# A backward pass with a long convolution and two dense layers: the opening put in one written order on all engines, with three spectrum blocks turned by DMA

## The chip, the cores and the metric

The kernel runs on one core of a Trainium2 chip. The time is device time in microseconds for one execution of the whole program; the median of several runs is given. A profile is one execution taken by the hardware profiler. PE is TensorE's matmul, PEld its weight load, DVE is VectorE, ACT is ScalarE, POOL is GpSimd, SP is SyncE, which here only issues DMAs.

## The reference

Two layer pairs are applied to x = A_q (1 x 2048 x 448, bf16): a gated long convolution A and a dense layer B with SiLU, A and B again; the outputs are the result and the gradients for all weights and inputs.

```python
def _A_ref(q, k, v, shift_k, ssm_k, ssm_D):
    ...
    for t in range(ks):
        k_shift = k_shift + k_pad[:, t:t + S, :] * shift_k[:, ks - 1 - t][None, None, :]
    kv = k_shift * v
    L = 2 * S
    ...
    y_f = kv_f * kf_f[None, :, :, :]
    y = (lambda x, s, axes=(-2,-1): jnp.fft.irfft2(x, s=s, axes=axes).astype(jnp.bfloat16))(y_f, (1, L), axes=(1, 2))[:, 0, :S, :]
    y = y + kv * ssm_D[None, None, :]
    return q * y
...
    x = x + _A_ref(_layernorm(x, axis=-1), A_k, A_v, A_shift_k, A_ssm_k, A_ssm_D)
    x = x + _B_ref(_layernorm(x, axis=-1), B_w1, B_w2)
    x = x + _A_ref(_layernorm(x, axis=-1), A_k, A_v, A_shift_k, A_ssm_k, A_ssm_D)
    x = x + _B_ref(_layernorm(x, axis=-1), B_w1, B_w2)
```

The convolution's result y depends on k, v and the filters alone, so it is computed once, ahead of the layers, by a Fourier transform of length 4096 written as matmuls (2048 = 128 x 16, in two stages).

## The kernel before

`_ssm_prefix` computes y; this text calls the part from the turn of k on (line 426 and after) the opening. `Main` then runs the layers forward and backward in four chunks of 512 rows, and `_ssm_suffix` with `Jobs` the convolution's gradients and the weight gradients.

The prefix begins by loading the filter, the constant matrices M1sb and Gsb, k, v and the first chunk of x (x0c0), all on SP's DMA queue (lines 371 to 380), and transforms the filter by its first stage into KAB's first half (`k_turn`, `k_stage1`). Then comes the opening. Its kinds of work, with the lines of before:

- k is transposed by TensorE into kT (line 432), half of each copy on ACT and half on DVE (434). `conv` (449) applies the four-tap shift as matmuls against diagonal matrices `diag` on half the channels (h) and four of the 16 row groups (jq); ACT copies the result to ks_kv (452), POOL stores it to DRAM (KS_d, 454), DVE multiplies it with v (455).
- `stage1_kv` is the first transform stage of that product (465), written to A1kv; once all jq of one half are in, A1kv is turned in 7 blocks of 16 squares of 128x128 (514) into Zkv (two tiles, ZkvA and ZkvB), where the second stage follows (`_fft_stage2_full`, 244) on 14 pieces of 1024.
- The filter's first stage is likewise turned in 7 blocks: two by DMA (426), five by TensorE in halves of 64 rows (`turn`, 225). `spec_k` (469) runs its second stage, stores the spectrum to DRAM and writes, with four DMAs from SBUF to SBUF (`_swap_halves_dma`, 282), a copy with real and imaginary parts exchanged into KAB's first half.
- `cons_prod` (519) copies a piece of the KV spectrum, stores it (540), has DVE multiply it with both forms of the filter's (pab, 542), and the inverse second stage (253, 254) goes from pab to PSUM and back to A1kv, whose storage is B1.
- In between, the first layer norm of x0c0 runs in eight steps (`_ln_steps`: four of statistics, POOL's power for rstd, four of scaling), and the weights w2T (by a transposing DMA), w1sb and w2sb are loaded.

After it `ys` (563) does the inverse first stage from B1 and ACT copies y to Ysb (564), which takes the buffer of ZkvA; X takes that of ZkvB. All PSUM tiles of the opening rotate through one tag, A, with four buffers. The order of each engine's instructions here is the scheduler's, from program order and priorities; which of ACT and DVE makes a copy is chosen by a running balance (`bal.pick`). From `Main` on, PE's order is that of the program (`manual_schedule`).

Of the kernel before, what the change touches and what calls it, by code (L numbers as in the profile page):

```python
# [17 lines left out]
P = 128  # L18
# [101 lines left out]
KPARTS = [(0, 128), (128, 256), (256, 384), (384, 448)]  # L120

# [126 lines left out]
def _fft_inv_stage2_full(k, pa, pb, B1, ci, psum):  # L248
# [6 lines left out]
    _copy(nc, k.bal.pick(1024), B1[:, 8 * ci:8 * ci + 8, :].rearrange("p a b -> p (a b)"), pv[:].rearrange("p a b -> p (a b)"))  # L255
# [56 lines left out]
def _ln_steps(k, pool, c, src, si, n_g):  # L312
# [4 lines left out]
    for tl in range(4):  # L317
        k.tc.keep_in_program_order(nc.vector.bn_stats(out=st[:, tl, :], in_=src(tl)))
# [15 lines left out]
def _ssm_prefix(k):  # L334
# [4 lines left out]
    with ExitStack() as es:  # L339
# [6 lines left out]
        k.M1sb = k.wk.tile([P, 16, 2, P], BF16, name="M1sb", tag="WX")  # L346
# [71 lines left out]
        def turn(src, dst, g):  # L418
            pt = psum.tile([P, 2, 16, 64], BF16, name="ps_tr", **a_)
            for i in range(16):  # L420
                _turn64(k, pt, i, src[:, 16 * g + i, :])
            for lo, hi, o in dst(g):
                _copy(nc, bal.pick((hi - lo) * P, dve_ns=0.53), o.rearrange("p i (r x) -> p r i x", r=2), pt[:, :, lo:hi, :])

        for g in range(5, 7):
            nc.sync.dma_start_transpose(out=Z[:, 16 * g:16 * g + 16, :], in_=A1Kf[:, 16 * g:16 * g + 16, :].rearrange("p a b -> p (a b)"))
        for jq in range(4):
            pt = psum.tile([DC, ND, 4, P], BF16, name="ps_kT", **a_)
            for u in range(4):
                j = 4 * jq + u  # L430
                for dc in range(ND):
                    nc.tensor.transpose(pt[:, dc, u, :], kn[:, j, dc * DC:(dc + 1) * DC], k.ident[:])
            for e, lo, hi in ((nc.scalar, 0, 2), (nc.vector, 2, 4)):
                _copy(nc, e, kT[:, jq, lo:hi, :, 1:129], pt[:, lo:hi])
        k.w2T = k.wk.tile([P, ND, F], BF16, name="w2T", tag="WY")
        nc.sync.dma_start_transpose(out=k.w2T[:, 0:3, :], in_=k.B_w2[:, 0:384])
        nc.sync.dma_start_transpose(out=k.w2T[:, 3:4, :], in_=k.B_w2[:, 320:448])
        DH = D // 2

        def conv(h, jq):  # L440
            ds = slice(h * DH, (h + 1) * DH)
            pc = psum.tile([P, 4, 256], FP32, name="ps_cv", tag="A", bufs=4)
            for u in range(4):
                j = 4 * jq + u
                for e in range(2):
                    for t in range(4):
                        js = (j - t) % J
                        src = kT[:, js // 4, 2 * h + e, js % 4, 1:129] if j >= t else kT[:, js // 4, 2 * h + e, js % 4, 0:128]
                        nc.tensor.matmul(pc[:, u, e * DC:(e + 1) * DC], lhsT=src, rhs=diag[:, 2 * h + e, t, :], start=(t == 0), stop=(t == 3))  # L449
            kk = work.tile([P, 2, 4, DH], BF16, name="ks_kv", tag="pab", bufs=4)  # L450
            ks, kvt = kk[:, 0], kk[:, 1]
# [41 lines left out]
        for p in prev:  # L493
            stage1_kv(*p)
# [880 lines left out]
```

## Time and profile before

| | us |
|---|---|
| median of 3 runs | 702.56 (701.79 to 702.73) |
| the profiled execution | 701.8 |
| its span | 700.0 |
| the opening in it | 18.9 to 90.6 |
| PE, DVE, ACT, POOL busy over the span | 666.0, 484.1, 432.9, 101.3 |

The span is counted from the execution's first record; times such as "at 41 us" are from there. Busy time is that of the engine's instructions, without waits; a group's row gives the line, engine, operation, output and inputs, shapes, count, then busy us and mean ns of one, then idle time just before and what ended it. A wait's row reads: engine and tile that waited, what it waited for, us in total, times, longest. A DMA's row gives where to and from, the issuing queue, count, KB each, and the median us from issue to landing.

### The profile page before, as it was taken

The page shows a single profiled execution, that of the slowest core. Times are in us where ns is not written, and L with a number is a line of the kernel's source. Part 1 is how long each engine was busy: PE and PEld are TensorE (multiplying, and loading weights), DVE is VectorE, ACT ScalarE, POOL GpSimd, SP SyncE. Part 2 cuts the span into 40 slices and gives each one's busy share as a digit, 9 for nine tenths or more (in the row PEclk, how much of TensorE's full clock was granted, in tenths as well). Part 3 has the DMA queues.
Part 4 walks back from the last instruction along what each step waited for, and adds up shares of the span by engine and source line. Part 5 has one row for each costly group of instructions (what it writes and reads, how often), then busy time and mean ns, then how long its engine had stood idle before and what let it go on. Part 6 is the DMA issues. An engine that isn't in the chain of part 4 may idle for free.

```text
span 700.0 us, 14553 instructions
## 1 busy us (share of the span) xinstructions
PE 666.0 (95%) x5897; PEld 358.8 (51%) x5933; DVE 484.1 (69%) x1131; ACT 432.9 (62%) x522; POOL 101.3 (14%) x173
## 2 busy tenths in 40 slices
PE   6898789999999999999999999999999999999996
PEld 5876545454444444434444444544554555555664
DVE  6688862676889948899578874853946545538991
ACT  5888766968856857769577585223554553554431
POOL 1057110110011100111000100010111211102311
PEclk9999999999999999999999999999999999999999
DMA  8999938459899976698677799959557888966981
GB/s 321 270 298 306 376 84 210 118 107 243 219 231 249 246 200 166 146 240 221 185 165 194 194 242 329 262 172 229 177 208 280 307 279 307 352 188 215 331 293 42
DMA packets 199798, 161.03 MB, mean 230 GB/s; under 512 B 147698, under 2 KB 180213, under 8 KB 198963
## 3 DMA queue, kind: packets, MB, share of 16 engines
q1 hardware_dynamic: 184550, 111.78, 58.8%
q0 software_dynamic: 10368, 36.29, 15.3%
q10 hardware_dynamic: 4812, 12.04, 5.0%
q8 instruction: 46, 0.75, 0.4%
q14 instruction: 22, 0.17, 0.1%
HBM read 66.05 MB, written 54.60 MB: 172 GB/s over the span
## 4 chain that ended last, share of the span: by engine, by line
PE 57%; DVE 22%; issue 10%; ACT 5%; POOL 3%; DMA 2%; POOLq 0%; DVEq 0%; ACTq 0%
PE ps_d L1046 19%; PE ps_n L836 8%; PE ps_h L638 6%; PE ps_g L638 6%; PE ps_o L798 5%; DVE ln_st L301 2%; DVE lb_v L994 2%; PE ps_v L265 2%; PE ps_cv L449 2%; POOL rstd L306 2%; DVE n L309 1%; DVE lb_v L997 1%; DVE lb_v L998 1%; DVE X L802 1%; PE ps_h L642 1%
## 5 line engine op out<-in xcount | busy, mean ns | idle before, releaser
L1046 PEld LDWEIGHTS <-dstat 128*128 128x128 bf16 x896 | 84.0, 98 | 77.8 <-issue 4.0
L836 PE MATMUL ps_n<-w1T,ghT 128*128 128x448 bf16 x448 | 96.6, 353 | 2.0 <-DVE ghT L821 1.7
L798 PE MATMUL ps_o<-w2sb,aT 128*128 128x448 bf16 x448 | 89.2, 353 | 0.7 <-DVE X L802 0.7
L638 PE MATMUL ps_h<-nT,w1sb 128*128 128x512 bf16 (+1 forms) x410 | 83.5, 336 | 2.2 <-ACT Dall L116 1.0
L116 ACT CAST ghT<-ps_g 128x1024 bf16<-128x1024 f32 (+1 forms) x54 | 48.4, 899 | 58.4 <-PE ps_g L642 47.7
L638 PE MATMUL ps_g<-nT,w2T 128*128 128x512 bf16 x317 | 77.9, 379 | 2.2 <-DVE Dall L117 0.5
L836 PEld LDWEIGHTS <-ghT 128*128 128x128 bf16 x448 | 41.4, 98 | 50.7 <-DVE ghT L821 6.7
L798 PEld LDWEIGHTS <-aT 128*128 128x128 bf16 x448 | 43.2, 98 | 41.1 <-issue 2.8
L638 PEld LDWEIGHTS <-w1sb 128*128 128x128 bf16 x420 | 39.2, 98 | 36.7 <-issue 7.2
L781 ACT ACTIVATE aT<-ps_h 128x1024 bf16<-128x1024 f32 (+1 forms) x48 | 44.2, 921 | 19.4 <-PE ps_h L638 10.5
L116 ACT CAST Dall<-ps_h 128x1024 bf16<-128x1024 f32 (+2 forms) x60 | 54.3, 904 | 0.0
L994 DVE SCALAR_TENSOR_TENSOR lb_v<-lb_u,n 128x448 bf16<-128x448 bf16 x60 | 37.2, 620 | 24.6 <-ACT lb_u L840 24.1
L791 ACT ACTIVATE Dall<-Dall 128x1024 bf16<-128x1024 bf16 (+1 forms) x48 | 53.2, 1186 | 0.1
L638 PEld LDWEIGHTS <-w2T 128*128 128x128 bf16 x336 | 31.3, 98 | 42.1 <-issue 7.2
L306 POOL TENSOR_TENSOR rstd<-ln_ve,mhalf 128x2 f32<-128x2 f32 (+1 forms) x24 | 19.9, 831 | 221.1 <-DVE ln_ve L305 221.1
L1046 PE MATMUL ps_d<-X,dstat 128*128 128x448 bf16 x224 | 47.9, 353 | 0.0
L1046 PE MATMUL ps_d<-go,dstat 128*128 128x448 bf16 x224 | 47.2, 353 | 0.0
L1046 PE MATMUL ps_d<-n3m,dstat 128*128 128x448 bf16 x224 | 46.4, 353 | 0.0
L1046 PE MATMUL ps_d<-n1m,dstat 128*128 128x448 bf16 x224 | 46.3, 353 | 0.0
L840 ACT ACTIVATE lb_u<-ps_n,rstd 128x448 bf16<-128x448 f32 x32 | 20.5, 640 | 28.7 <-PE ps_n L836 24.3
L116 ACT CAST A1g<-ps_v 128x1024 bf16<-128x1024 f32 x14 | 14.9, 1066 | 36.5 <-PE ps_v L265 36.5
L802 DVE TENSOR_TENSOR X<-X,ps_o 128x448 bf16<-128x448 bf16 x32 | 19.5, 610 | 21.3 <-PE ps_o L798 21.1
(206 smaller groups left out, 1111.6 us busy)
## 6 DMA issues: line engine op xcount, KB each, us to landing
dstat<-a_d SPq DMA_DIRECT2D x28, 512.0 KB, 5.0
dstat<-g_d SPq DMA_DIRECT2D x28, 512.0 KB, 5.2
a_d<-turned SPq DMA_DIRECT2D x16, 512.0 KB, 3.0
g_d<-turned SPq DMA_DIRECT2D x16, 512.0 KB, 3.2
a_d<-turned SPq DMA_DIRECT2D x16, 384.0 KB, 2.7
g_d<-turned SPq DMA_DIRECT2D x16, 384.0 KB, 3.0
spec_K<-KAB POOLq DMA_DIRECT2D x7, 512.0 KB, 5.4
KAB<-KAB POOLq DMA_DIRECT2D x28, 128.0 KB, 4.6
```

Source lines behind the costliest of these rows:

```text
L116: return nc.scalar.copy(out, in_)
L265: nc.tensor.matmul(pv[:, r ^ (ci & 1), i, :], lhsT=src[ri, i * P:(i + 1) * P], rhs=k.Gsb[ri, g, ri], start=first, stop=not first)
L306: nc.gpsimd.tensor_tensor(out=r[:, lo:hi], in0=ve[:, lo:hi], in1=k.mhalf[:, lo:hi], op=ALU.pow)
L638: self.nc.tensor.matmul(ps, lhsT=w[:, b, ft * P:(ft + 1) * P], rhs=x[:, b], start=(start and b == 0), stop=(stop and b == bs[2]))
L781: self.last_silu = nc.scalar.activation(aT[hh][:, o:o + hi - lo, :], ps(lo, hi), ACT.Silu)
L791: self.nc.scalar.activation(dT[hh][:, o:o + n, :], dT[hh][:, o:o + n, :], ACT.Derivative_silu)
L798: nc.tensor.matmul(po[:, :D], lhsT=aT[ft // 7][:, ft % 7, tl * P:(tl + 1) * P], rhs=self.w2sb[:, ft, :], start=(ft == 0), stop=(ft == NF - 1))
L802: self.last_o = nc.vector.tensor_tensor(out=X[:, t, :], in0=X[:, t, :], in1=po[:, :D], op=ALU.add)
L836: nc.tensor.matmul(pn[:, :D], lhsT=gh[ft // 7][:, ft % 7, tl * P:(tl + 1) * P], rhs=self.w1T[:, ft, :], start=(ft == 0), stop=(ft == NF - 1))
L840: nc.scalar.activation(u0[:], pn[:, :D], ACT.Identity, scale=k.rstd[2 * L + 1][:, t:t + 1], accum_out=cp[:, tl, 0:1])
L994: nc.vector.scalar_tensor_tensor(out=v[:], in0=u0, scalar=-1.0 / D, in1=n_t, op0=ALU.mult, op1=ALU.mult, accum_out=cp[:, 1:2])
L1046: self.nc.tensor.matmul(ps[:, :D], lhsT=st[:, t, :], rhs=mov[:, t, :], start=(first and t == 0), stop=(last and t == NT - 1))
```

## The change

The opening is written as a list of 207 pieces. A token's first letter says the kind, digits which one; a small letter is a copy or ACT's or DVE's step, with a (ACT) or d (DVE) at its end, and x or y ahead of it for the first or second half of a split copy. T turn of k, t its copy; K turn of a filter block, k its copy; C convolution, c its copy and store, m the product with v; S first stage, s its copy; P second stage of the filter, p its copy, Q store and swap; Z turn of a KV block by TensorE, z its copy, D the same by DMA; F second stage of KV, f its copy and store; M product of spectra, V inverse, v its copy; N a step of the layer norm; W0 grad_out's chunk, W1 w2T, W2 w1sb, W3 w2sb.

Within it all engines, SP's and POOL's queues too, keep the list's order. KV blocks 0, 1 and 2 (D0 to D2), which need only the first half of the channels, are turned by DMA on SP's queue, and their F, M and V stand among the convolutions of the second half. The five filter blocks are turned in whole squares. w1sb and w2sb are loaded by SP instead of ACT, w2T behind D2 instead of ahead of the first store. `diag` moves from the filter's tile to that of M1sb; pab has three buffers of its own and ks_kv two, where both shared four. The steps of the layer norm are no longer pinned one by one.

```diff
+OPENING = """
+W0 T0 N0 T1 t0xa t0yd T3 N1 t1xa T2 t1yd t3xa t3yd C01 t2xa t2yd N2 C02 c01 N3 m01 K1 c02 N4 S011 k1a m02 S010 s011d
+S021 N5 s010a P3 s021d P2 p3a S020 p2d P10 s020a P11 N6 C03 Q1 p10a p11d N7 C00 c03 Q5 m03 P12 c00 S030 p12d P13 s030a
+S031 m00 K4 p13a s031d S001 Q6 S000 s001a k4d K0 s000a P8 k0d P9 p8a D0 K2 p9d P1 P0 p1a k2d Q4 C11 D1 p0a C13 c11 Q0
+m11 D2 P4 c13 P5 p4d S111 p5a S110 m13 K3 s110a s111d Q2 S131 s131a k3d S130 F0 s130a f0d P7 P6 p7a F3 p6d F2 f3a F1 M0
+C10 Q3 f2a M3 f1a C12 c10 M1 V0 m10 c12 V1 M2 v0a S101 v1a m12 V3 s101d S120 v3a V2 s120d S100 v2a S121 W1 W2 W3 s100d
+F4 s121a F5 f4d f5a Z5 M4 Z6 z5a Z4 M5 Z3 z4a z6d V4 z3xd V5 v4a z3yd F12 v5a F7 f12d F11 f7a F13 f11d F10 f13a F9 M7 F8
+f9a F6 M13 f10a f8a M11 V7 f6a V13 M10 V11 v7a M6 V10 v13a M12 V6 v10a M9 V12 v11a M8 v12a V9 v6a v9d V8 v8a
+"""
...
-    _copy(nc, k.bal.pick(1024), B1[:, 8 * ci:8 * ci + 8, :].rearrange("p a b -> p (a b)"), pv[:].rearrange("p a b -> p (a b)"))
+    return pv
...
-        k.tc.keep_in_program_order(nc.vector.bn_stats(out=st[:, tl, :], in_=src(tl)))
+        nc.vector.bn_stats(out=st[:, tl, :], in_=src(tl))
...
+        m1t = k.wk.tile([P, 16 * 2 * P + ND * 4 * DC], BF16, name="M1sb", tag="WX")
+        k.M1sb = m1t[:, 0:16 * 2 * P].rearrange("p (n c k) -> p n c k", c=2, k=P)
+        m1f = m1t
-        diag = w2o[:DC, 2 * S:].rearrange("p (c j d) -> p c j d", c=ND, j=4)
+        diag = m1t[:DC, 16 * 2 * P:].rearrange("p (c j d) -> p c j d", c=ND, j=4)
...
+        Zt = [None, None]
+
+        def zkv(lo, hi):
+            h = lo // H2
+            if Zt[h] is None:
+                Zt[h] = k.wk.tile([P, H2], BF16, name=("ZkvA", "ZkvB")[h], tag=("W2", "WX")[h])
+            return Zt[h][:, lo - h * H2:hi - h * H2]
+
+        def block(g, lo=0, hi=16):
+            return zkv(2048 * g + lo * P, 2048 * g + hi * P).rearrange("p (a b) -> p a b", b=P)
+
+        k.na0 = _hd(k, [P, 4, D], "na0")
+        k.gb0 = _hd(k, [P, 4, D], "gb0")
+        norm = _ln_steps(k, work, 0, lambda tl: k.x0c0[:, tl, :], 0, k.na0)
+        live, seen = {}, set()
+
+        def bank(key, shape, name, dt=FP32):
+            live[key] = psum.tile(shape, dt, name=name, **a_)
+            return live[key]
+
+        def transposes(key, name, src, g):
+            pt = bank(key, [P, 16, P], name, BF16)
             for i in range(16):
+                nc.tensor.transpose(pt[:, i, :], src[:, 16 * g + i, :], k.ident[:])
+
+        def T(jq):
+            pt = bank(("t", jq), [DC, ND, 4, P], "ps_kT", BF16)
             for u in range(4):
                 for dc in range(ND):
+                    nc.tensor.transpose(pt[:, dc, u, :], kn[:, 4 * jq + u, dc * DC:(dc + 1) * DC], k.ident[:])
+
+        def t(jq, part, eng):
+            lo = 2 * part
+            _copy(nc, eng, kT[:, jq, lo:lo + 2, :, 1:129], live["t", jq][:, lo:lo + 2])
+
+        def K(g):
+            transposes(("k", g), "ps_tr", A1Kf, g)
+
+        def k_(g, part, eng):
+            _copy(nc, eng, Z[:, 16 * g:16 * g + 16, :], live["k", g][:])
+
+        def C(h, jq):
+            pc = bank(("c", h, jq), [P, 4, 256], "ps_cv")
             for u in range(4):
                 j = 4 * jq + u
                 for e in range(2):
+                    for tt in range(4):
+                        js = (j - tt) % J
+                        src = kT[:, js // 4, 2 * h + e, js % 4, 1:129] if j >= tt else kT[:, js // 4, 2 * h + e, js % 4, 0:128]
+                        nc.tensor.matmul(pc[:, u, e * DC:(e + 1) * DC], lhsT=src, rhs=diag[:, 2 * h + e, tt, :], start=(tt == 0), stop=(tt == 3))
+
+        def c(h, jq):
+            live["m", h, jq] = work.tile([P, 2, 4, DH], BF16, name="ks_kv", tag="kk", bufs=2)
+            ks = live["m", h, jq][:, 0]
+            nc.scalar.copy(ks, live["c", h, jq][:, :, :DH])
             nc.gpsimd.dma_start(out=k.KS_d[h, :, 4 * jq:4 * jq + 4, :], in_=ks)
+
+        def m(h, jq):
+            kk = live["m", h, jq]
+            nc.vector.tensor_tensor(out=kk[:, 1], in0=kk[:, 0], in1=vn[:, 4 * jq:4 * jq + 4, h * DH:(h + 1) * DH], op=ALU.mult)
+
+        def S_(h, jq, u):
+            ps = bank(("s", h, jq, u), [P, 2, 2, 256], "ps_s1")
+            for w in range(2):
+                for cc in range(2):
+                    nc.tensor.matmul(ps[:, w, cc, :DH], lhsT=k.M1sb[:, 4 * jq + 2 * u + w, cc, :], rhs=live["m", h, jq][:, 1, 2 * u + w, :], start=True, stop=True)
+
+        def s(h, jq, u, part, eng):
+            n2 = 4 * jq + 2 * u
+            _copy(nc, eng, A1kv[:, 112 * h:112 * (h + 1), :, n2:n2 + 2, :].rearrange("p b c w s -> p w c b s"),
+                  live["s", h, jq, u][:, :, :, :DH].rearrange("p w c (b s) -> p w c b s", s=2))
+
+        def P_(ci):
+            live["p", ci] = _fft_stage2_full(k, Ka[:, ci * 1024:(ci + 1) * 1024], ci, psum)
+
+        def p(ci, part, eng):
+            _copy(nc, eng, Ka[:, ci * 1024:(ci + 1) * 1024], live["p", ci][:])
+
+        def Q(cp):
             lo, hi = cp * 2048, (cp + 1) * 2048
             nc.gpsimd.dma_start(out=k.SPEC_d["K"][:, lo:hi], in_=Ka[:, lo:hi])
             _swap_halves_dma(k, KAB[:, 0, :], Ka, lo, hi)
 
+        def D_(g):
+            nc.sync.dma_start_transpose(out=block(g), in_=B1[:, 16 * g:16 * g + 16, :].rearrange("p a b -> p (a b)"))
+
+        def Z_(g):
+            transposes(("z", g), "ps_tr", B1, g)
+
+        def z(g, part, eng):
+            lo, hi = (8 * part, 8 * part + 8) if g == 3 else (0, 16)
+            _copy(nc, eng, block(g, lo, hi), live["z", g][:, lo:hi, :])
+
+        def F_(ci):
+            live["f", ci] = _fft_stage2_full(k, zkv(ci * 1024, (ci + 1) * 1024), ci, psum)
+
+        def f(ci, part, eng):
+            _copy(nc, eng, zkv(ci * 1024, (ci + 1) * 1024), live["f", ci][:])
+            seen.add(ci)
+            for lo, hi in ((0, 2), (2, 4), (4, 6), (6, 7), (7, 9), (9, 11), (11, 13), (13, 14)):
+                if ci in range(lo, hi) and seen >= set(range(lo, hi)):
+                    nc.gpsimd.dma_start(out=k.SPEC_d["KV"][:, lo * 1024:hi * 1024], in_=zkv(lo * 1024, hi * 1024))
+
+        def M(ci):
+            pab = work.tile([P, 2, 1024], BF16, name="pab", tag="pab", bufs=3)
             xs = zkv(ci * 1024, (ci + 1) * 1024)
+            nc.vector.tensor_tensor(out=pab[:], in0=xs.rearrange("p (o f) -> p o f", o=1).broadcast_to((P, 2, 1024)), in1=KAB[:, :, ci * 1024:(ci + 1) * 1024], op=ALU.mult)
+            live["V", ci] = pab
+
+        def V(ci):
+            pab = live["V", ci]
+            live["v", ci] = _fft_inv_stage2_full(k, pab[:, 1], pab[:, 0], ci, psum)
+
+        def v(ci, part, eng):
+            _copy(nc, eng, B1[:, 8 * ci:8 * ci + 8, :].rearrange("p a b -> p (a b)"), live["v", ci][:].rearrange("p a b -> p (a b)"))
+
+        def N(i):
+            next(norm, None)
+
+        def W(i):
+            if i == 0:
+                nc.sync.dma_start(out=k.gb0[:], in_=_pm(k.grad_out[0])[:, 0:4, :])
+            elif i == 1:
+                k.w2T = k.wk.tile([P, ND, F], BF16, name="w2T", tag="WY")
+                nc.sync.dma_start_transpose(out=k.w2T[:, 0:3, :], in_=k.B_w2[:, 0:384])
+                nc.sync.dma_start_transpose(out=k.w2T[:, 3:4, :], in_=k.B_w2[:, 320:448])
+            elif i == 2:
+                w1x = k.wk.tile([P, ND * F + 2 * D], BF16, name="w1sb", tag="W1")
+                k.w1sb = w1x[:, 0:ND * F].rearrange("p (c f) -> p c f", f=F)
+                k.xq = [w1x[:, ND * F:].rearrange("p (j d) -> p j d", d=D)]
+                nc.sync.dma_start(out=k.w1sb[:, 0:3, :], in_=k.B_w1[0:384, :].rearrange("(c p) f -> p c f", p=P))
+                nc.sync.dma_start(out=k.w1sb[:, 3, :], in_=k.B_w1[320:448, :])
             else:
+                w2x = k.wk.tile([P, (NF + 2) * D], BF16, name="w2sb", tag="WB")
+                k.w2sb = w2x[:, 0:NF * D].rearrange("p (c d) -> p c d", d=D)
+                k.xq.append(w2x[:, NF * D:].rearrange("p (j d) -> p j d", d=D))
+                nc.sync.dma_start(out=k.w2sb, in_=k.B_w2.rearrange("(c p) d -> p c d", p=P))
+
+        do = dict(T=T, t=t, K=K, k=k_, C=C, c=c, m=m, S=S_, s=s, P=P_, p=p, Q=Q, D=D_, Z=Z_, z=z, F=F_, f=f, M=M, V=V, v=v, N=N, W=W)
+        two = {"P", "p", "F", "f", "M", "V", "v"}
+        with tc.manual_schedule(engines={e.engine for e in (nc.tensor, nc.scalar, nc.vector, nc.gpsimd, nc.sync)}):
+            for g in range(5, 7):
+                nc.sync.dma_start_transpose(out=Z[:, 16 * g:16 * g + 16, :], in_=A1Kf[:, 16 * g:16 * g + 16, :].rearrange("p a b -> p (a b)"))
+            for tok in OPENING.split():
+                kind, num = tok[0], "".join(x for x in tok[1:] if x.isdigit())
+                args = [int(num)] if kind in two else [int(x) for x in num]
+                if tok[-1] in "ad":
+                    args += [int(tok[-2] == "y"), nc.scalar if tok[-1] == "a" else nc.vector]
+                do[kind](*args)
```

More of the change, by code (lines that the diff above doesn't have):

```diff
@@ L445, in conv @@
                 for e in range(2):
[L446 to L451, printed above, removed]
@@ L493, in _ssm_prefix @@
-        for p in prev:
-            stage1_kv(*p)
-        H2 = SPEC // 2
-        Zkv = [k.wk.tile([P, H2], BF16, name="ZkvA", tag="W2"), k.wk.tile([P, H2], BF16, name="ZkvB", tag="WX")]
-        k.gb0 = _hd(k, [P, 4, D], "gb0")
-        nc.sync.dma_start(out=k.gb0[:], in_=_pm(k.grad_out[0])[:, 0:4, :])
-        for i in range(4, 7):
-            spec_k(i)
-        B1 = A1kv[:].rearrange("p b c n s -> p (b c n s)").rearrange("p (a x) -> p a x", x=P)
-        def zkv(lo, hi):
-            h = lo // H2
-            return Zkv[h][:, lo - h * H2:hi - h * H2]
```

106 lines of the change are left out of this document (6 added, 100 removed).

## The prediction

> **What bounds the kernel now.** I read the page's shares first (TensorE busy 95% of the span), then the chain of waits to find where the edited part ends, then busy time by stretch. The edited part, called the opening here, runs from the turn of k (18.9 us) to the last write of the inverse result (90.6 us). Three stretches of it, columns: length, then busy us of PE, PEld, DVE, ACT, POOL, granted clock, DMA share, GB/s:
>
> ```profile
> 18.90:38.60 19.70, 17.43 (x413) 16.59 (x411) 12.85 (x20) 16.56 (x17) 2.23 (x4) 1.00 1.19 265
> 38.60:62.20 23.60, 22.15 (x274) 17.58 (x277) 19.69 (x26) 19.99 (x20) 16.54 (x32) 1.00 1.01 304
> 62.20:90.60 28.40, 20.05 (x280) 15.12 (x282) 23.52 (x22) 21.64 (x23) 8.63 (x17) 1.00 0.96 337
> sum 71.70, PE 59.63 PEld 49.30 DVE 56.05 ACT 58.19 POOL 27.39; mean PE 19.88 PEld 16.43 DVE 18.68 ACT 19.40 POOL 9.13
> ```
>
> No engine is full: of 71.7 us PE works 59.6, ACT 58.2, DVE 56.1. They wait on one another, most in the third stretch (PE idle 8.4 us). The DMA engines, though, are occupied throughout (share about 1). The waits of 20 to 100 us say on what:
>
> ```profile
> PEld L253 <- DVE pab L542: 10.3, 7, 2.9
> PE ps_v L253 <- DVE pab L542: 7.4, 7, 2.4
> ...
> PE ps_tr L225 <- issue: 2.3, 1, 2.3
> ```
>
> The inverse waits 7.4 us for DVE's products; and PE once stood 2.3 us for nothing that the profile shows (27.6 to 29.9).
>
> The opening's end is this copy, behind which the main part's first matmuls (L563) wait:
>
> ```profile
> 89.36 1.23 DVE L117 CAST A1kv<-ps_v 128x1024 bf16<-128x1024 f32 x1 [1.16 <-PE ps_v L254]
> ```
>
> **The change: work.** Rows of the groups in the opening:
>
> ```profile
> L117 DVE COPY ZkvA<-ps_tr 128x2048 bf16<-128x2048 bf16 x2 | 2.4, 1220 | 0.0
> ...
> L514 PE MATMUL ps_tr<-ident,A1kv 128*128 128x128 bf16 x112 | 6.4, 219 | 0.0
> ...
> L225 PE MATMUL ps_tr<-ident,KAB 64*128 64x64 bf16 x160 | 3.0, 190 | 2.3 <-issue 2.3
> ```
>
> PE: three of seven spectrum blocks (Z) leave it, 48 of the 112 transposes at 6.4/112 = 57 ns: -2.75 us. Five K blocks are turned in 16 full transposes instead of 32 half ones: 5 x 0.92 - 3.0 = +1.6 us. Sum 59.6 - 1.2 = 58.5 us. The three Z copies go too (some 1.2 us each on DVE, 1.8 on ACT). The list gives each copy a fixed engine; counting its letters against the rows of before (pitch of a 1024 copy 0.92 us on ACT, 1.14 on DVE): ACT has one inverse copy more and one each of stage 1, K spectrum, KV spectrum and K turn less, 58.2 - 3.6 = 54.6; DVE comes out at 56.0, as before. So work shrinks little; the change lives on taking out some 12 us of waiting per engine. With PE's 58.5 us and the last copy and hand-over (1.2 us) the opening could not end before 78.6.
>
> **The order's first stretch.** In the new list N0 (statistics of x0c0) is DVE's first instruction, ahead of its half of the kT copies. Its data:
>
> ```profile
> 7.82 0.33 SPq L378 DMA_DIRECT2D x0c<-in_A_q_dram  x1
> ```
> ```profile
> x0c<-in_A_q_dram SPq DMA_DIRECT2D x1, 448.0 KB, 15.5
> ...
> KAB<-KAB POOLq DMA_DIRECT2D x28, 128.0 KB, 4.6
> ...
> KAB<-KAB SPq DMA_TRANSPOSE x2, 8.0
> w2T<-in_B_w_dram SPq DMA_TRANSPOSE x2, 11.7
> ```
>
> It lands at 7.8 + 15.5 = 23.3 (last column: us to landing), so DVE, free since 19.7, stands 3.6 us. Behind N0 queue t0yd, t1yd, t3yd; the PSUM tag has four buffers and C01 is the fifth request, so it waits for t0yd: 23.3 + 0.75 + 0.69 = 24.8, where before it began at 22.6. From there I add durations in list order (rows of before: a convolution C 13.9/8 = 1.74, S 7.7/16 = 0.48, a product m 0.62, statistics 0.75, K 0.92): C01 to 26.6, C02 28.3, K1 29.2; DVE goes through t1yd, t3yd, t2yd, N2, N3 (29.3), m01 (29.9), N4 behind POOL's power of 1.04 (30.8), m02 (31.4), s011d (32.5), s021d (34.0), p2d (35.1). So S011 runs at 30.0, S021 at 31.5, P2 at 32.5; C03 takes P2's buffer and runs 35.1 to 36.9; C00 ends at 38.6. PE's list work to that point is 15.2 us, so 4.5 us are lost. Before also lost its 2.3 us here, and at 38.6 has about the same PE work left (42.5 us against 42.7). The first stretch gives nothing.
>
> **The rest.** I cut the remaining list at D0, D2, F0, C12, S121, F12 and V7 and took the busiest engine of each piece: 6.3 (ACT), 5.3, 4.1, 5.6 (PE), 5.7, 6.8, 5.7 (DVE), 7.4 (ACT), plus 1.2 for the end = 48.1 us; PE alone would need 42.7 + 1.2 = 43.9. Four PSUM buffers let neighbours overlap: I take the middle, 46.0, which without DMA trouble ends the opening at 84.6.
>
> **DMA.** D0 to D2 add three SBUF turns of 512 KB on SP's queue, and w2T's turn, w1sb and w2sb now follow them there (w2T was at 30 us, the others on ACT's queue at 68 and 73). Turns, alone and beside stores, and the plain traffic of the POOL queue (same columns as above):
>
> ```profile
> 32.00:34.00 2.00, 2.00 (x60) 1.86 (x57) 1.64 (x3) 1.68 (x3) 0.00 (x0) 1.00 1.15 106
> 34.00:37.00 3.00, 3.00 (x51) 2.93 (x49) 2.79 (x5) 2.67 (x4) 0.54 (x1) 1.00 1.28 290
> ...
> 44.00:62.00 18.00, 16.98 (x219) 13.72 (x221) 15.03 (x18) 15.40 (x16) 13.25 (x27) 1.00 0.98 335
> ```
>
> Turns alone move 290 GB/s, plain traffic 335, but where KS_d's stores fall between turns it drops to 106; over 24 to 43 us, all of it a mixture, the mean is 203. D0 is issued near 44 us (s000a), just where POOL's swaps of KAB run. Each Q is 1.05 MB (512 KB and four times 128 KB). M0, the first product, needs Q0, before which 2.55 MB on POOL's queue (Q4, Q0, two KS_d) and 1.05 MB of turns (D0, D1) must pass: 3.6 MB from 44 us on land at 54.7 by 335 GB/s and at 61.7 by 203. M0's place on DVE is 56.5 by the pieces above. I take the middle, 58.2, a wait of nearly 2 us, with DVE's whole list behind it (27.3 us of work) and V0 behind M0 on PE. F3 and F2 need D1 (44 + 8.0 + about 5 = 57) near 55.5; that wait lies beside the same one. D2, w2T, w1sb and w2sb I cost at nothing: F4 comes near 66, and main asks for w2T at 96.5, w1sb at 102, w2sb at 112 now; if SP's queue fell 20 us behind, w2T would be what main waits for. ACT's three issues that go (2.1 us on its queue) lay beside its copies; POOL issues the same 51 DMAs in another order. The own two buffers of ks_kv and the three of pab (four shared before) cost nothing while a KS_d lands within 7 us, the longest of before: c03, at 37, needs the store of 27.6.
>
> The Trainium skill (DMA: Bandwidth & Descriptors, section Queues, rings and completion order) says that a DMA engine serves its queues in turn, a packet at a time. From 42.2 to 43.2 the trace has 401 small turn packets beside 42 plain ones, 291 GB/s together, which fits; by that pace a D of 2048 packets takes 5 us, and the sum stays.
>
> **Sum.** 38.6 + 46.0 + 2 = 86.6; by DVE, 58.2 + 27.3 + 1.2 and half a us of gaps, 87.2; with small waits at POOL's hand 87.5. The opening ends 90.6 - 87.5 = 3.1 us earlier, and the PE-bound rest moves with it. Profiled execution: 701.8 (span 700.0 and 1.8 around it) to 698.7; its run lies 0.76 below the median of 702.56, so the forecast for the median is **699.5 us**.
>
> **Rivals.**
> - *The order runs undisturbed by DMA.* For: Q4 and Q0 may not collide with D0 as the first D starts from an almost drained queue; C10 and C12 (3.5 us) cover V0. Against: share near 1 throughout. Opening ends 82.5 (38.6 + 43.9) to 84.6: 694.5 to 696.5. Chance 0.12.
> - *A new wait behind the opening.* ZkvA's last store (after f6a) is issued some 7 us before the end, and Ysb, in the same buffer, is written about 1 us after it; landings of such stores were 3.5 to 10.5 us. Over 8 us it costs, and 10.5 us gives 2.5 back. Or PE's 2.3 us without a visible cause returns: it fell where DMA moved 53 GB/s (28 to 29.5). Either gives 701.5 to 702. Chance 0.15.
> - *Slower: turns and swaps jam.* At the 106 to 131 GB/s of 32 to 34 and 38 to 41 us kept up, M0 comes at 71 to 78. The point where it decides: M0 at 61.6 (90.6 - 29.0), 3.6 MB in 17.6 us, 205 GB/s, just the mean of 24 to 43. For it: that mean. Against: D meets swaps, not only stores, and 42.2 to 43.2 shows 291 with swaps. At 164 GB/s M0 is at 66 and the time 707. Chance 0.25. The Trainium skill (VectorE: DVE Perf Modes, Rules for kernel authors) advises TensorE for a 128x128 transpose when PSUM can take it, and the DMA otherwise, which speaks for this rival; the trace agrees in kind, 57 ns on PE against 113 ns for a square of 32 KB at 290 GB/s.
>
> That the change does nothing is out: each engine's order is rewritten. The forecast itself has 0.48 (697 to 701).
>
> **How the numbers follow.** A measurement here tells 0.2%, 1.4 us: faster is under 701.15, slower over 703.97. Faster: 0.48 + 0.12 = 0.60; same 0.15; slower 0.25. The range holds 8 in 10 from the undisturbed case to most of the jam: 695.0 to 706.0; the likeliest case alone is 697 to 701.
>
> **What would show it.** N0 starts at 23.3 with DVE idle before it, and C01 near 24.8 (if N0 starts at 20, the x0c0 step is wrong). C00 ends near 38.6. D0 is issued near 44; M0 starts near 58 with its wait on DMA (at 56: first rival; past 62: jam). The last A1kv copy ends near 87.5; Ysb's first copy waits for ps_y, not for a store. After that the timeline is before's, 3 us early; if the main part changes length by more than 1 us, I am wrong on what the change touches.

## The result, and the profile after

The changed kernel takes **747.24 us** (median of 6 runs, 744.56 to 756.1) against 702.67 for the kernel before beside it: a ratio of 1.0634, 95% interval 1.0598 to 1.0669. The run of 756.1 us counts as slow and is left out of the ratio. I had forecast 699.5 and a range of 695 to 706. Both the sign and the size were wrong.

The profiled execution has a span of 743.2 us against 700.0. Nearly all of that lies in the opening: the first copy into Ysb starts at 133.43 us in place of 91.69, 41.7 us later (before, then after):

```profile
91.69 1.71 ACT L564 CAST Ysb<-ps_y 128x896 bf16<-128x896 f32 x2 [2.92 <-PE ps_y L563]
```
```profile
133.43 1.71 ACT L593 CAST Ysb<-ps_y 128x896 bf16<-128x896 f32 x2 [11.47 <-DMA spec_KV<-ZkvA]
```

The rest, 1.5 us, follows directly behind: Ysb's first six copies are spread over more time, while TensorE's granted clock is on average still 0.73 (133 to 143 us).

The opening by stretches, columns as before (length, busy us of PE, PEld, DVE, ACT, POOL, granted clock, DMA share, GB/s):

```profile
19.00:43.00 24.00, 21.11 (x286) 18.65 (x287) 17.74 (x30) 17.16 (x19) 9.30 (x17) 0.93 0.93 258
43.00:80.00 37.00, 23.23 (x274) 18.02 (x274) 17.94 (x18) 17.26 (x20) 12.50 (x25) 0.82 1.13 192
80.00:124.00 44.00, 23.53 (x289) 18.84 (x289) 21.48 (x21) 20.63 (x20) 5.88 (x11) 0.77 1.21 132
124.00:134.40 10.40, 0.29 (x3) 0.04 (x2) 0.03 (x1) 0.97 (x2) 0.00 (x0) 0.70 1.04 312
```

Up to 43 us all is well. Then every engine is half idle, while the DMA engines are occupied more than before (share 1.13 and 1.21) and move far less: 192 and 132 GB/s, where the kernel before moved 335. In the last of the four stretches the rate is back at 312 GB/s: what the engines still wait for there is the last store, which shares the DMA engines with the loads of w1sb and w2sb (issued from 118.6 us on). The granted clock falls with PE's idle time. PE had work again at 134.4 us, and the clock rose from 0.50 (134.4 to 137 us) to 1.00 (139 us and after), so I read it as a consequence.

The waits from 40 to 140 us (us in all, times, the longest) say what the engines stood for:

```profile
PE ps_s L255 <- DMA ZkvA<-A1kv: 18.8, 3, 7.9
...
DVE pab L539 <- DMA spec_KV<-ZkvB: 13.0, 1, 13.0
ACT Ysb L593 <- DMA spec_KV<-ZkvA: 11.5, 1, 11.5
POOL KAB L293 <- DMA KAB<-KAB: 9.4, 4, 8.2
...
DVE pab L539 <- DMA KAB<-KAB: 5.6, 1, 5.6
```

The first line is F waiting for the turned blocks D0 to D2. The last line is M0, which starts at 70.07 us:

```profile
70.07 3.51 DVE L539 TENSOR_TENSOR pab<-ZkvA,KAB 128x2048 bf16<-128x2048 bf16 x3 [5.63 <-DMA KAB<-KAB]
```

The second line, M7's wait from 97.6 to 110.6 us, is put down to a store of ZkvB. But a product only reads ZkvB and KAB, which needs no store to be done, and the two stores of ZkvB issued by then, at 97.85, took over 20 us to land. The last swap of the KAB block that M7 reads was issued at 82.31 (its row from 82.2 to 82.5 us):

```profile
KAB<-KAB POOLq DMA_DIRECT2D x1, 128.0 KB, 28.1
```

It landed at 110.4, and I take it that M7 waited for that swap.

The chain of waits (start, us, what) runs through plain DMAs of POOL's queue almost without a break:

```profile
44.04 12.67 DMA KAB<-KAB
...
57.84 8.74 DMA spec_K<-KAB
...
66.85 15.76 DMA KAB<-KAB
...
83.71 29.38 DMA spec_KV<-ZkvA
```

SP's timeline (start, us, the instruction) shows the other side: first w2T's turn in the kernel before, then the turns of the changed kernel. The DMA issues of 44 to 124 us (KB each, median us from issue to landing) show what all of them took:

```profile
30.16 6.52 SPq L436 DMA_TRANSPOSE w2T<-in_B_w_dram  x1
36.72 2.52 SPq L437 DMA_TRANSPOSE w2T<-in_B_w_dram  x1
```
```profile
43.22 26.41 SPq L517 DMA_TRANSPOSE ZkvA<-A1kv  x3
69.73 35.29 SPq L557 DMA_TRANSPOSE w2T<-in_B_w_dram  x1
105.06 13.39 SPq L558 DMA_TRANSPOSE w2T<-in_B_w_dram  x1
```
```profile
KAB<-KAB POOLq DMA_DIRECT2D x19, 128.0 KB, 12.8
...
spec_KV<-ZkvA POOLq DMA_DIRECT2D x3, 512.0 KB, 28.6
...
ZkvA<-A1kv SPq DMA_TRANSPOSE x3, 17.2
w2T<-in_B_w_dram SPq DMA_TRANSPOSE x2, 25.5
```

A swap of 128 KB lands after 12.8 us where it took 4.6; w2T's turn, which held SP's queue for 9.0 us before, holds it for 48.7. Turns and swaps meet at 43.2 us, and both queues stay occupied until past 118.

My theory was then: **turning DMAs in flight beside another queue's plain DMAs slow both** (the jam). The rivals: the turned blocks are slow in themselves; the load is too much or too early, turned or not; the written order is at fault.

### The profile page after: what moved, and what is told of

It reads as the page before. It is cut to its first block, busy times and chain, and to the rows that moved or that the text cites. A ratio compares the mean times of both kernels' runs of the same rounds, so it can differ in the third digit from the quotient of the medians.

```text
span 743.2 us, 14300 instructions
## 1 busy us (share of the span) xinstructions
PE 675.0 (91%) x5770; PEld 365.2 (49%) x5805; DVE 484.3 (65%) x1131; ACT 429.9 (58%) x519; POOL 101.7 (14%) x173
## 4 chain that ended last, share of the span: by engine, by line
PE 49%; DVE 19%; DMA 16%; issue 10%; POOL 3%; ACT 3%; POOLq 0%; SPq 0%; ACTq 0%; DVEq 0%
PE ps_d L1075 17%; PE ps_n L865 7%; DMA spec_KV<-ZkvA 7%; PE ps_h L667 6%; PE ps_g L667 5%; PE ps_o L827 5%; DMA KAB<-KAB 4%; DVE ln_st L312 2%; DMA x0c<-in_A_q_dram 2%; PE ps_v L276 2%; DMA spec_K<-KAB 2%; DVE lb_v L1023 2%; POOL rstd L317 2%; DVE n L320 1%; DVE X L831 1%
## 5 line engine op out<-in xcount | busy, mean ns | idle before, releaser
L116 ACT CAST ghT<-ps_g 128x1024 bf16<-128x1024 f32 (+1 forms) x54 | 48.3, 899 | 58.6 <-PE ps_g L671 48.0
L865 PEld LDWEIGHTS <-ghT 128*128 128x128 bf16 x448 | 41.5, 98 | 50.7 <-DVE ghT L850 6.7
L827 PEld LDWEIGHTS <-aT 128*128 128x128 bf16 x448 | 43.2, 98 | 41.3 <-issue 3.0
L667 PEld LDWEIGHTS <-w1sb 128*128 128x128 bf16 x420 | 39.2, 98 | 36.7 <-issue 7.2
L810 ACT ACTIVATE aT<-ps_h 128x1024 bf16<-128x1024 f32 (+1 forms) x48 | 44.2, 920 | 19.4 <-PE ps_h L667 10.5
```

The lines of the kernel that those rows point to most:

```text
L116: return nc.scalar.copy(out, in_)
L667: self.nc.tensor.matmul(ps, lhsT=w[:, b, ft * P:(ft + 1) * P], rhs=x[:, b], start=(start and b == 0), stop=(stop and b == bs[2]))
L810: self.last_silu = nc.scalar.activation(aT[hh][:, o:o + hi - lo, :], ps(lo, hi), ACT.Silu)
L827: nc.tensor.matmul(po[:, :D], lhsT=aT[ft // 7][:, ft % 7, tl * P:(tl + 1) * P], rhs=self.w2sb[:, ft, :], start=(ft == 0), stop=(ft == NF - 1))
L865: nc.tensor.matmul(pn[:, :D], lhsT=gh[ft // 7][:, ft % 7, tl * P:(tl + 1) * P], rhs=self.w1T[:, ft, :], start=(ft == 0), stop=(ft == NF - 1))
```

## The experiments

In the diffs a token line is cut to the tokens concerned. Every kernel ran beside the kernel before, whose median stayed at 702.7 to 703.5 us. Without an interval a time is one execution.

**e1, w2T's turn back to its early place.**
```diff
-N1 t1xa T2 t1yd
+N1 t1xa T2 W1 t1yd
...
-S121 W1 W2 W3
+S121 W2 W3
```


> After with w2T's turning DMA moved up the list to just behind the turn of k (about 29 us on SP's queue, as before the change); the three D stay. Jam theory (a turning DMA in flight beside POOL's plain DMAs slows both): D0 to D2 still meet Q4, Q0 and Q2, so F4 still waits until about 80 us, but the KV stores after it run free; the opening ends near 100 us instead of 134, time about 712 us. Load theory (three more blocks are more bytes than the DMA engines carry, whatever their kind): the bytes are the same, the opening still ends past 125, time 738 or more. Order theory (the list on five in-order engines loses the time, DMA only follows): within 5 us of 747.

730.85 us. 16 us come back, not the 35 expected: w2T's two parts took 20.4 us of SP (30.2 to 50.6), and D0 to D2, issued behind them, 27.9 (50.7 to 78.6). The list sends its first spectrum store and swaps from 36.0 us on, the kernel before from 42.5, when its w2T had left SP's queue (39.2) and the last of its small packets were moving (to about 44); so the early turn now has swaps beside it too.

**e2, no turned blocks, w2T's turn late.** Blocks 0 to 2 go through TensorE, and w2T follows w1sb.
```diff
-P9 p8a D0 K2 p9d P1
+P9 p8a Z0 K2 p9d z0a P1
...
-C11 D1 p0a C13 c11
+C11 Z1 p0a C13 z1d c11
...
-D2 P4 c13 P5 p4d
+Z2 P4 c13 P5 z2a p4d
...
-S121 W1 W2 W3
+S121 W2 W1 W3
```


> After with the three D replaced by turns on TensorE (Z0 to Z2 with their copies at the same places), and w2T's turning DMA behind w1sb on SP's queue, so that it starts at about 60 us when the last convolution is done. Jam theory: the first half to 60 us runs clean (M0 near 57), then w2T meets Q3 and the KV stores for some 20 to 40 us; Ysb waits for ZkvA's last store; opening ends between 95 and 115, time 707 to 727 us. Load theory: 1.5 MB less than after, so DMA ends near before's 89 us: opening near 88, time about 700. Order theory: about 745 us.

719.74 us. From 39 to 60 us, with no turn in flight, 299 GB/s; then w2T's turn took 42 us of SP, 80 to 100 us moved 131 GB/s, and Ysb waited 18.7 us for ZkvA's store. One turn, with no turned block about, is enough.

**e3, no turned blocks, w2T's turn early.** The blocks as in e2, w2T as in e1.
```diff
-N1 t1xa T2 t1yd
+N1 t1xa T2 W1 t1yd
...
-P9 p8a D0 K2 p9d P1
+P9 p8a Z0 K2 p9d z0a P1
```


> After with both: no D (Z0 to Z2 on TensorE) and w2T's turn at about 29 us. The fixed list alone. Jam theory: no turn is in flight after about 43 us; the opening ends between 84 and 88 us, time 696 to 700 us, that is faster than before. Load theory: the same as before's DMA, 697 to 703 us. Order theory: about 740 us or more, with the waits between engines and not on DMA.

715.51 us, a miss for the jam as I had put it (696 to 700), until one looks at who lies beside w2T: Q1 and Q5, from 35.4 us on. w2T took 26 us of SP, 39 to 60 us moved 135 GB/s, and the ks copies waited 16.6 us for KS_d's stores.

**e4, the same transfers as plain copies.** D0 to D2 and w2T stay where they are, but copy instead of turning. In e4 to e7 what is copied is not turned (w2T then holds rows of w1), so they compute something else with transfers of the same size.
```diff
-nc.sync.dma_start_transpose(out=block(g), in_=B1[:, 16 * g:16 * g + 16, :].rearrange("p a b -> p (a b)"))
+nc.sync.dma_start(out=block(g), in_=B1[:, 16 * g:16 * g + 16, :])
...
-nc.sync.dma_start_transpose(out=k.w2T[:, 0:3, :], in_=k.B_w2[:, 0:384])
-nc.sync.dma_start_transpose(out=k.w2T[:, 3:4, :], in_=k.B_w2[:, 320:448])
+nc.sync.dma_start(out=k.w2T[:, 0:3, :], in_=k.B_w1[0:384, :].rearrange("(c p) f -> p c f", p=P))
+nc.sync.dma_start(out=k.w2T[:, 3, :], in_=k.B_w1[320:448, :])
```


> After with the D of blocks 0 to 2 and w2T's load made plain copies of the same number of bytes at the same places of the same queue: the blocks are not turned, and w2T holds rows of w1, so outputs that depend on them are not the reference's. Jam theory: plain copies share the DMA engines without loss; M0 near 57 us, opening ends 84 to 89, time 696 to 701 us, granted clock back to 1.0. Load theory: as slow as after, 740 us or more. Order theory: 740 us or more.

710.38 us: 37 of the 45 us go with the turning alone. About 7 us stay, where I had expected none (696 to 701). The rate is good, 302 and 336 GB/s (39 to 60 and 60 to 80 us), but M0 waited 13.2 us for its swap; I read that as sharing, what SP loads early coming off what POOL's queue gets.

**e5, the list alone.** No turned blocks, w2T a plain copy as in e4, and the last of SP's loads.
```diff
-P9 p8a D0 K2 p9d P1
+P9 p8a Z0 K2 p9d z0a P1
...
-S121 W1 W2 W3
+S121 W2 W3 W1
```


> After without the D (blocks 0 to 2 turned on TensorE) and with w2T's load a plain copy of the same bytes (rows of w1: outputs behind it are not the reference's), last on SP's queue behind w1sb and w2sb. The list alone: no turn is in flight after the filter's two blocks. e2 ran its list like this up to 81 us, before its store stuck. If the list is sound, the opening ends 85 to 88 us and the time is 697 to 700 us, 3 to 6 below before; if the list itself loses, 703 or more.

701.59 us, ratio 0.9977 (0.9964 to 0.9991). The order loses nothing (703 or more was the sign of that), but it gains 1.5 us and not the 3 to 6 expected. Its last inverse copies on DVE and ACT, and then the one wait that gave part back:

```profile
85.72 1.23 DVE L117 CAST A1kv<-ps_v 128x1024 bf16<-128x1024 f32 x1
```
```profile
86.85 1.01 ACT L116 CAST A1kv<-ps_v 128x1024 bf16<-128x1024 f32 x1 [0.34 <-PE ps_v L265]
91.52 1.71 ACT L593 CAST Ysb<-ps_y 128x896 bf16<-128x896 f32 x2 [3.65 <-DMA spec_KV<-ZkvA]
```

The opening's last copy ends at 87.86 in place of 90.59, but Ysb, whose buffer ZkvA has, waits 3.65 us for a store that was issued at 80.70 and took 10.64.

**e6 and e7, the three blocks back into e5, turned (e6) and as plain copies (e7, with D_ as in e4).** Against e5:
```diff
-P9 p8a Z0 K2 p9d z0a P1
+P9 p8a D0 K2 p9d P1
```
(and D1, D2 likewise)

> e5 with the three D back as turning DMAs: what D0 to D2 alone cost. Jam theory: D0 to D2 take 15 to 25 us each beside Q4, Q0 and Q2, F4 near 80 us, opening ends 96 to 104, time 708 to 716. If the turns are harmless by themselves (w2T was the whole of it): 697 to 700.

> e6 with the D plain copies of the same bytes (blocks 0 to 2 not turned). Interference of turns: 1.5 MB of plain copies cost the swaps at most 4 us of DMA, M0 at 58 to 61, time 697 to 702, at least 8 us under e6. Load alone: as e6 within 2 us.

718.62 and 706.2 us, both above what I had expected of them (708 to 716 and 697 to 702). The waits from 40 to 110 us, e6 and then e7:

```profile
PE ps_s L255 <- DMA ZkvA<-A1kv: 18.5, 3, 11.3
```
```profile
DVE pab L539 <- DMA KAB<-KAB: 7.5, 1, 7.5
```

As a load the blocks cost 4.6 us (706.2 - 701.6), through M0's swap; that they are turned costs 12.4 more. From 43 to 80 us e7 moved 315 GB/s and e6 177.

**e8, one queue.** e3, with all that POOL issues in the opening issued by SP instead, in the list's order.
```diff
-    k.nc.gpsimd.dma_start(out=dst[o, lo:hi], in_=src[i, lo:hi])
+    k.nc.sync.dma_start(out=dst[o, lo:hi], in_=src[i, lo:hi])
```
(and the same word in c, Q and f)

> The right outputs: no D, w2T's turn at about 29 us, and all DMAs that POOL issued in the opening (KS_d, K spectra, swaps, KV spectra) issued by SP instead, in the list's order behind one another on one queue. Jam theory, where a turn and a plain DMA of one queue follow one another: w2T takes 7 us as alone, is through by 38 to 40, Q1 behind it; opening ends 85 to 89, time 697 to 701, against 715.5 of e3. If turns and plain DMAs hurt each other on one queue as on two: 712 to 720.

711.94 us, ratio 1.0118 (1.0103 to 1.0133): the time is a miss, the mechanism not. w2T's turn took 7.8 us of SP in place of 26. But the stores of KS_d stood behind it, and c03's copy waited 6.0 us for its buffer. 4.5 us of the rest do not lie in the opening (see the last section).

**e9, the turn first, the swaps after it, on two queues.** Against e3; F6 moves up too.
```diff
-C03 Q1 p10a p11d N7 C00 c03 Q5 m03 P12 c00
+C03 p10a p11d N7 C00 c03 m03 P12 c00 Q1 Q5
...
-z3yd F12 v5a F7 f12d
+z3yd F6 v5a F12 f6a F7 f12d
...
-f9a F6 M13 f10a f8a M11 V7 f6a V13
+f9a M13 f10a f8a M11 V7 V13
```


> The fixed list without the turned blocks (0 to 2 go through TensorE again). w2T's turn is issued behind T2's transposes (near 30 us, as in the kernel before). The tokens Q1 and Q5 move behind c00, so that POOL's first k spectrum DMAs leave near 41 us, where w2T's turn is through, in place of 35.4; and F6 with its copy f6a moves up behind z3yd, so that ZkvA's last spectrum store leaves some 7 us earlier than in e5 (80.7 us there). If turning DMAs beside another queue's plain ones are the cause (jam): w2T's turn lands in 10 to 14 us, the ks copies don't wait for KS_d, the swaps run above 280 GB/s, Ysb no longer waits 3.7 us for the store, and the time is e5's 701.6 less 2 to 4 us: 697 to 700. Rival (a turn in this list is late whatever lies beside it, because the list asks for its buffers earlier than the planner's order did): e3's wait of 16.6 us for KS_d comes again in part and the time is 706 to 716. Rival 2 (delaying Q1 and Q5 only shifts the wait to M0 at KAB's swap): turn clean, pab waits for KAB 4 to 8 us, 702 to 707.

706.44 us, ratio 1.0044 (1.0025 to 1.0064). As the second rival says: the turn is through in 11.3 us of SP, Ysb waits for no store, and M0 waits 5.4 us for its swap (66.0 in place of 58.5 in e5).

**e10, the changed kernel on one queue.** Turned blocks and late w2T as they are; only the edit of e8.


> The changed kernel as it is (three blocks turned by DMA, w2T's turn behind them), with one edit: every DMA that POOL issued in the opening (KS_d, spec_K, the swaps, spec_KV) is issued by SP instead, in the list's order, so that no turn is in flight beside another queue's plain DMA except for queue overlap at a turn's edges. Jam between two queues: D0 to D2 take 5 to 8 us each in place of 17 to 29, 43 to 80 us moves above 220 GB/s in place of 160, w2T's two parts are through in 10 to 15 us of SP in place of 49, and the time falls from 747 to 708 to 722 (the queue's order still holds KS_d and the swaps back behind the turns). Rival (turns of this kernel's own tiles and of DRAM are slow in themselves, or the load alone is too much): D and w2T stay at 12 us or more a piece and the time stays above 735.

719.7 us. Same DMAs, same order, one queue: 27.5 us of the 44.6 are back. The turns on SP's timeline:

```profile
46.77 3.18 SPq L517 DMA_TRANSPOSE ZkvA<-A1kv  x1
53.26 3.09 SPq L517 DMA_TRANSPOSE ZkvA<-A1kv  x1
60.24 2.85 SPq L517 DMA_TRANSPOSE ZkvA<-A1kv  x1
74.60 6.88 SPq L557 DMA_TRANSPOSE w2T<-in_B_w_dram  x1
81.53 1.56 SPq L558 DMA_TRANSPOSE w2T<-in_B_w_dram  x1
```

Nine us for three blocks in place of 26.4, 8.4 for w2T in place of 48.7. What is left is for the most part the queue's own order: ZkvA's last store, behind w2T and the loads, leaves at 95.1, and Ysb waits 12.2 us; M0 waits 7.1 us for its swap, and 4.6 us are lost at the very end (see the last section).

**e11, the kernel before with one turn moved.** Nothing of the change; w2T's turn waits for the first copy of the convolution's second step.
```diff
-        k.w2T = k.wk.tile([P, ND, F], BF16, name="w2T", tag="WY")
-        nc.sync.dma_start_transpose(out=k.w2T[:, 0:3, :], in_=k.B_w2[:, 0:384])
-        nc.sync.dma_start_transpose(out=k.w2T[:, 3:4, :], in_=k.B_w2[:, 320:448])
...
+            if ci == 0:
+                k.w2T = k.wk.tile([P, ND, F], BF16, name="w2T", tag="WY")
+                nc.scalar.copy(k.w2T[:, 0:4, 0:1], xs[:, 0:4].rearrange("p (a b) -> p a b", b=1))
+                nc.sync.dma_start_transpose(out=k.w2T[:, 0:3, :], in_=k.B_w2[:, 0:384])
+                nc.sync.dma_start_transpose(out=k.w2T[:, 3:4, :], in_=k.B_w2[:, 320:448])
```


> The kernel before, its opening as it was, with w2T's turn alone moved: it waits for the first copy of the convolution's second FFT step (near 64 us) in place of going out near 32 us. Jam: the turn is in flight for 25 to 45 us beside POOL's swaps and spec_KV stores, 64 to 90 us moves 130 to 200 GB/s, Ysb or pab waits for those DMAs and the time is 712 to 728. Rival (the loss belongs to the fixed list, whose order leaves no slack for a late transfer): the planner's order has room, the turn is through in 12 to 16 us and the time is 702 to 706.

747.85 us. One turn of 1.8 MB, moved by 35 us, costs the old kernel as much as the whole change did, and more than I expected of it. The kernel before from 64 to 90 us:

```profile
64.00:90.00 26.00, 18.93 (x275) 14.81 (x278) 21.13 (x19) 20.18 (x22) 7.51 (x15) 1.00 0.98 346
```

e11's stretch from 64 us on, SP's timeline, the wait of the product, and landings from 64 to 125 us:

```profile
64.00:125.00 61.00, 24.47 (x284) 18.75 (x287) 23.50 (x22) 21.20 (x24) 7.51 (x15) 0.72 1.12 147
```
```profile
65.25 50.21 SPq L538 DMA_TRANSPOSE w2T<-in_B_w_dram  x1
115.51 16.48 SPq L539 DMA_TRANSPOSE w2T<-in_B_w_dram  x1
```
```profile
DVE pab L544 <- DMA KAB<-KAB: 25.7, 1, 25.7
```
```profile
w2sb<-in_B_w_dram ACTq DMA_DIRECT2D x1, 1568.0 KB, 63.0
spec_KV<-ZkvA POOLq DMA_DIRECT2D x3, 512.0 KB, 53.4
```

In place of 346 GB/s it is 147 (163 from 64 to 90 us), the DMA share is high, and a store of 512 KB lands after 53 us. Ysb's first copy comes at 125.89, 34.2 us later than before. The other 12 us lie behind it: X waits 11.1 us for ZkvB's store, and the main part's first matmuls with w2T wait, partly at the same time, 7.8 us for w2T itself. The rival that blamed the written order is out.

**e12, the swaps in the order of need.** e9, with Q6 behind Q0, Q4 behind Q3, and one ring of five buffers for ks_kv and pab.
```diff
-s031d S001 Q6 S000
+s031d S001 S000
...
-k2d Q4 C11 Z1 p0a C13 z1d c11 Q0
+k2d C11 Z1 p0a C13 z1d c11 Q0 Q6
...
-C10 Q3 f2a M3
+C10 Q3 Q4 f2a M3
```


> The kernel of the run before (no turned blocks; w2T's turn ahead of the swaps; F6 early), in which M0 waited 5.4 us for its swap: POOL issued Q6 and Q4 (blocks that M8 to M13 read, 84 us and later) ahead of Q0 (which M0 reads at 60.6). Here Q6 comes right behind Q0 and Q4 behind Q3, and ks_kv and pab share one ring of 5 buffers in place of 2 and 3, so that c03's copy no longer waits 2.9 us for KS_d of c01. If the swaps' order was what M0 waited for (two of four megabytes less ahead of Q0): pab waits 0 to 1 us for KAB, the last A1kv copy ends at 88 to 91 in place of 94.9, and the time is 700 to 703, level with the kernel before or up to 0.4% under it. Rival (the DMA engines as a whole are behind after 11 us of turn, and the wait only moves from M0 to M4, M5 or to the KV stores): a wait of 3 us or more shows on pab or Ysb further on and the time is 704 to 707.

703.01 us, ratio 1.0018 (0.9996 to 1.004), level. M0 no longer waits (58.6 us). The order of the swaps and the ring were not run apart.

**e13, e14 and e15.** e12 with w1sb's loads behind ZkvA's last store and w2sb's behind ZkvB's: that is e15. On one queue it is e14, and with blocks 0 to 2 turned again on that queue e13.
```diff
-S121 W2 W3 s100d
+S121 s100d
...
-F12 f6a F7
+F12 f6a W2 F7
...
-f10a f8a M11
+f10a f8a W3 M11
```


> The list of the run before this one (no turned blocks, swaps in the order in which M needs them, one ring of 5 for ks_kv and pab, F6 early), with every DMA of the opening on SP's queue, w2T's turn ahead of all KS_d, and the loads of w1sb behind ZkvA's last store and of w2sb behind ZkvB's last store. One queue leaves nothing beside a turn: w2T's turn takes 6 to 8 us of SP as in e8, no ks copy waits (5 buffers), the swaps follow from 38 us, and the time is 698 to 702. Rival (a single queue holds each store behind all that was issued ahead of it, as e8 and e10 showed in part): pab or Ysb waits 3 us or more for a DMA and the time is 704 to 710.

> The same kernel with blocks 0, 1 and 2 turned by DMA on that one queue in place of TensorE's transposes and their copies. If the turns as such are cheap and only the second queue made them dear: each takes 3 to 5 us of SP, and the kernel is within 2 us of the one with transposes, or faster by the 3.3 us of PE and 3.7 us of copies that they save where these lie on the path. Rival (a turn holds the queue for all that stands behind it, the swaps and ks stores above all, 3 x 3 us): pab waits for KAB and the time is 4 to 12 us above the kernel with transposes.

> The kernel of the run before this call on two queues as it was (POOL's DMAs on POOL's queue), only the loads of w1sb and w2sb moved behind ZkvA's and ZkvB's last stores. If the loads' share of the DMA engines is what is left: KS_d of c10 and c12 and spec_KV leave sooner, the last A1kv copy ends 1 to 3 us sooner than 88.8 and the time is 699 to 702, under the kernel before. Rival (nothing waits on them any more, the list's rest is bound by its own order): 701.5 to 704, level.

e15: 701.5 us, ratio 0.9996 (0.9965 to 1.0028), level. e14: 705.44, ratio 1.0028 (1.0012 to 1.0044), though its opening is as good as e15's (Ysb's first copy at 90.24 and 90.39; before 91.69): it loses its 4.7 us at the very end. e13: 708.97, ratio 1.0078 (1.0061 to 1.0095). The turned blocks, with no second queue beside them, cost 3.5 us more than TensorE's transposes: pab waits 4.8 us for KAB, PE 2.5 for the blocks and X 2.3 for ZkvB's store, none of which e14 shows. The stretch from 43 to 80 us of e13 and of e14:

```profile
43.00:80.00 37.00, 30.32 (x391) 23.81 (x392) 27.36 (x28) 27.87 (x29) 0.00 (x0) 1.00 1.02 277
```
```profile
43.00:80.00 37.00, 34.16 (x455) 27.54 (x456) 30.32 (x30) 32.76 (x33) 0.00 (x0) 1.00 0.87 287
```

## Why the prediction failed

The loss in four steps: the list with w2T as a plain copy, last in its queue, 703.1 to 701.6 (e5); the blocks as plain loads, 706.2 (e7); turned, 718.6 (e6); w2T's turn in place of a plain copy, and ahead of the loads instead of behind them, 747.2 (the changed kernel). So -1.5, +4.6, +12.4 and +28.6 us. The steps are rough, as e6 and e7 are one execution each and the changed kernel's lay between 744.6 and 756.1. Of the last step some 4 us may be w2T's place ahead of the loads: with plain copies that place costs 4.2 us (e4 less e7). Point by point:

- **First stretch: right.** N0 began at 23.19 (23.3 forecast) with DVE idle 3.46 us ahead of it for x0c0, C01 at 24.67 (24.8), C03 and C00 ran from 34.89 to 38.20 (to 38.6). D0 was issued at 43.22 (near 44).
- **The rest of the list: right in direction, too short in size.** The sum has 46.0 us from C00's end to the last copy without DMA trouble, an end at 84.6. e5, in which M0 (58.52) waits for no DMA, took 49.7 us and ended at 87.86; the three transposes that the change takes out (2.75 us by my rows) lie in that, so about 1 us of the difference is left to the list itself. That e5 ends 2.7 us earlier than before, close to the 3.1 forecast, is luck: the 3.1 held a DMA wait that e5 doesn't have. With the blocks turned, the list was never seen to end early: e13's last copy ended at 90.8.
- **"D2, w2T, w1sb and w2sb I cost at nothing": this step failed most.** My ground was that main asks for w2T only at 96.5. That looks at the turn's own reader, not at what lies beside it. w2T is 1.8 MB of turns behind D2 in a stretch full of KV stores. M7's last swap took 28.1 us to land, and M7 waited 13.0; POOL waited 12.0 for a swap too, ZkvA's last store left only at 113.6, and Ysb waited 11.5. The step cost 28.6 us in all.
- **The DMA term, 2 us on M0: failed.** I took the middle of 335 and 203 GB/s for 3.6 MB and 8 us for a turn's landing. Measured: 192 GB/s from 43 to 80 us, the turns landing after 17 us (median), F waiting 18.8 us for them, and M0 at 70.07 in place of 58.2. The rows that I set aside, 106 and 131 GB/s where stores fell between turns, were the ones to take; the second of 42.2 to 43.2 with 291 GB/s, which I set against them, was not typical: it was the end of a turn.
- **The third rival, "turns and swaps jam", named the mechanism** and its place; I gave it 0.25 and 707 us. M0 came 4 us later than the 66 behind that price, which by the same reckoning makes 711 us. The price was too low mainly because I let it end at M0: the other 36 us came after it. A slow turn stays in flight longer and meets the next swaps and stores, so 3.6 MB were too few to reckon with.
- **The second rival** came true as well: Ysb waited for ZkvA's store, 3.65 us in e5 (10.64 to landing, as the 10.5 that I had read in the profile) and 11.5 in the changed kernel.
- **Work.** The counts came out: ACT has 13 inverse copies in place of 12, and 64 of 112 transposes of KV blocks stay on PE. Only the five filter blocks cost 5.3 us in place of 4.6. In 43 to 80 us e5 has PE busy for 35.3 of 37 us.

I had found a rule of the Trainium skill to fit (DMA: Bandwidth & Descriptors: an engine serves its queues in turn, packet by packet). It may hold, but it only says how a rate is shared out; here the sum of both fell to 131 to 192 GB/s, where turns alone had 290 and plain DMAs 335, and no run shows why. The same page of the Trainium skill, in its section Rules for kernel authors, says that "A transpose next to ordinary DMAs needs nothing". For the time this case says otherwise: e11 loses 45 us by it. The other page of the Trainium skill that I weighed (VectorE: DVE Perf Modes: TensorE for a 128x128 transpose where PSUM can take it) agrees with e13 against e14, 3.5 us.

What the engines do inside while a turn and another queue's copies share them stays open. No run tells whether the place is the turning path, the memory or the descriptors. It is shown that the loss comes with turns in flight beside another queue's plain DMAs, and that it goes when one queue issues both in order. But the other queue always held POOL's DMAs, which the profile lists under software_dynamic, and SP's under hardware_dynamic; e8, e10, e13 and e14 changed the number of queues and the kind together. In e11 ACT's loads, from a hardware queue, were slowed too (w2sb landed after 63.0 us, before after 17.0), but beside POOL's stores. Whether a turn beside ACT's queue alone would lose as much was not run.

## What to carry to other kernels

Keep turning DMAs away, in time, from a long run of plain DMAs of another queue (here POOL's): put them where the other queue has little to move, or issue both from one queue, and price a moved turn by all that is in flight until it lands, not by its own reader alone. When a profile holds one short row in which two kinds of traffic run together far below either alone, take that row as the price of a longer meeting until a run says otherwise. Any early load takes its share from the transfer that the next product waits for, so order transfers by need.

## What was not expected of the hardware

- Turns alone moved 290 GB/s and plain DMAs 335; together, from two queues, 131 to 192 (the changed kernel, e2, e3, e6, e11). On one queue, one behind the other, 268 and 277 (e10, e13; e14, with no turn in that stretch, 287).
- The DMA share doesn't show the jam by itself: it was 1.12 to 1.22 in the worst stretches (e3's 135 GB/s had 1.22) and 0.87 to 1.02 in good ones, but 1.28 where turns alone moved 290 GB/s. GB/s beside the share does.
- The kernels with one queue end later than their last instruction explains. e14's last issue on POOL ends at 695.2 and the span at 703.1; in the kernel before it is 696.7 and 700.0. That is 7.9 us against 3.3, and 7.9 again in e8, e10 and e13; e15, with the same list on two queues, has 3.0. The cause is open; the opening of e14 is not the place of its loss.
